# A planned attention and MLP block: LayerNorm in other VectorE forms, more time allowed for DMA transposes, score packs that may go out in halves

## The chip, the cores and the metric

One core of a Trainium2 chip. The metric is device time in microseconds (us). Most executions of one kernel agree within 0.3%. Engines: PE (TensorE), ACT (ScalarE), DVE (VectorE), POOL (GpSimd), SP (issues DMAs).

## The reference

```python
x = A_x                                             # 1 x 2048 x 640, bf16
h  = x + attention(layernorm(x), wq, wk, wv, wo)    # 32 heads of 20, one shared k and v
h2 = h + (gelu(ln(h) @ w_gate) * (ln(h) @ w_up)) @ w_down        # Df = 1536
```

Layernorm has no learned scale; eps is 1e-5. Attention is full: 32 heads x 2048 x 2048 scores.

## The kernel before

The program is written by a planner: it keeps an assumed clock for each engine, asks whichever engine is free first what to do next, and so fixes the order of every queue. What the chip runs is that order, with semaphores; the assumed times are gone. Two things follow. Every assumed duration changes the order, and a queue that was ordered for a too early arrival stands still behind it.

Scores are made in packs: four matmuls, one per 32-row group, each filling one PSUM bank (128 x 512). A tile of scores then goes one of two ways. ACT takes an exponential, one bank or two adjacent ones at a time. Or DVE writes a bit-pattern approximation ("DVE tile" below), which POOL completes with two shifted copies, so that it costs PE three value matmuls, not one.

```python
# a DVE instruction in a two-port mode and any POOL instruction exclude each other (the planner's view)
def commit(self, eng, fn, cost, lat, ..., lock=False):
    ...
    if lock:
        for o in self.ops["pool"][-2:]:
            if o.t0 <= t0 < o.end:
                t0 = o.end
        self.port = t0 + cost
    elif eng == "pool":
        t0 = max(t0, self.port)

# LayerNorm: after bn_stats/bn_aggr -> mv[..., 0] mean, mv[..., 1] variance
dve(lambda e: e.tensor_copy(ln_vb[:, ln, sl], mv[:, ln, sl, 1]), 80, ...)
dve(lambda e: e.tensor_scalar_add(ln_veb[:, ln, sl], ln_vb[:, ln, sl], EPS), 80, ...)
# ... POOL: pow 0.5; DVE: reciprocal ...
tk = _Task(("dve",), None, 320, L_DVE, keys + [("lr", kk)], [], prio, then, gate)
tk.lock = True
tk.fn = lambda e: e.tensor_scalar(xn_tmp[:, s, :], xh[:, t, :], mv[:, ln, t, 0:1],
                                  ln_r[:, ln, t:t + 1], ALU.subtract, ALU.mult)
sp_tasks.append(_Task(("sp",), lambda e: e.dma_start_transpose(o, xn_tmp[:, s, :]), 1330, 1700, ...))

# POOL stays idle up to YIELD ns for a locked DVE task that is about to be ready
if YIELD and state["kv_left"] == 0 and plan.free["dve"] < t + YIELD: ...   # for tk in tasks: if tk.lock ...

# a pack of scores needs four free banks; n of its four tiles go to DVE
if cand and len(ok) >= 4:
    issue_qk(t, cand[0], cand[1], ok)
# in issue_qk:
elif Dv > TH0: n = 0
elif Dv < SP2D[ph] and len(pend[1]) + len(pend[2]) < 2 * SP2P[ph] and (
        stall(t, 1, fb) + 1382.0 - stall(t, 2, fb) - 956.0 > SP2G[ph]): n = 2
else: n = 1
```

The softmax here doesn't subtract the row's maximum and nothing guards it: scores larger than these inputs give would overflow.

Of the kernel before, what the change touches and what calls it, by code (L numbers as in the profile page):

```python
# [9 lines left out]
P = 128  # L10
_DEBUG = {}
# [208 lines left out]
def bass_sequential_preLN__grouped_kv_mqa__glu_gated_geglu__prompt_kernel(  # L220
# [38 lines left out]
    EVF = 0  # L259
    EVW = 200.0  # L260
# [7 lines left out]
    NQ = 4  # L268
    NXT = 4
# [21 lines left out]
    qT = sb("qT", [P, NQ, 512], BF16)  # L291
    kT4 = sb("kT4", [P, S], BF16)
# [18 lines left out]
    ln_vb = sb("ln_vb", [P, 2, NT], BF16)  # L311
    ln_veb = sb("ln_veb", [P, 2, NT], BF16)
    ln_denb = sb("ln_denb", [P, 2, NT], BF16)
# [39 lines left out]
    SP2P = (3, 3, 3)  # L353
    SP2G = (300.0, 300.0, 300.0)
# [17 lines left out]
    YIELD = 500.0  # L372
    WQA = 1
    W_LAT = 3000.0
    ADDW = 100.0
# [7 lines left out]
    load("sp", xh[:, 0, :], x_view[:, 0, :], [("x", 0)], 2000)  # L383
# [19 lines left out]
    pool(lambda e: e.memset(halfc[:], 0.5), 40, writes=["halfc"])  # L403
    pool(lambda e: e.memset(wk4[:].bitcast(F32), 0.0), 300, writes=["wk4z"])
# [12 lines left out]
    state = {"mode": "m", "tab": "exp", "npack": 0, "exps_left": 2048, "misc_ready": False, "kv_left": NT, "qk_left": 512}  # L417
    bank_owner = {b: None for b in range(8)}
    slots = {"xt": list(range(NXT)), "q": list(range(NQ)), "onT": list(range(4)), "osb": [0, 1], "rcp": [0, 1], "onr": [0, 1]}
# [26 lines left out]
    def ln_group(ln, tiles, prio, done):  # L446
# [5 lines left out]
        def after_stats(op):  # L452
            cnt[0] += 1
            if cnt[0] == n:
                dve(lambda e: e.tensor_copy(ln_vb[:, ln, sl], mv[:, ln, sl, 1]), 80,
                    [("mv", ln, t) for t in tiles], [("vb", kk)], prio, c2)

        def c2(op):
            dve(lambda e: e.tensor_scalar_add(ln_veb[:, ln, sl], ln_vb[:, ln, sl], EPS), 80,
                [("vb", kk)], [("veb", kk)], prio, c3)  # L460

        def c3(op):
            task(("pool",), lambda e: e.tensor_tensor(ln_denb[:, ln, sl], ln_veb[:, ln, sl], halfc[:, 0:n], ALU.pow),
                 780, L_POOL, [("veb", kk), "halfc"], [("den", kk)], prio, c4)

        def c4(op):
            dve(lambda e: e.reciprocal(ln_r[:, ln, sl], ln_denb[:, ln, sl]), 90, [("den", kk)], [("lr", kk)],
                prio, c5)
# [5 lines left out]
        def norm(t):  # L474
# [9 lines left out]
            def then(op):  # L484
# [19 lines left out]
                sp_tasks.append(_Task(("sp",), lambda e: e.dma_start_transpose(o, xn_tmp[:, s, :]), 1330, 1700,  # L504
# [3 lines left out]
            tk = _Task(("dve",), None, 320, L_DVE, keys + [("lr", kk)], [], prio, then, gate)  # L508
            tk.lock = True

            def bind():
                s = start()
                tk.fn = lambda e: e.tensor_scalar(xn_tmp[:, s, :], xh[:, t, :], mv[:, ln, t, 0:1],  # L513
                                                  ln_r[:, ln, t:t + 1], ALU.subtract, ALU.mult)
                tk.writes = [("xt", s)]
# [73 lines left out]
    def kv_job(tiles):  # L589
# [24 lines left out]
        def vthen(b):  # L614
# [3 lines left out]
            def vfin(op):  # L618
                free_bank(b)
                for w in (1, 2):  # L620
                    task(("pool",), (lambda w: lambda e: e.tensor_scalar(
                        v_ext[:, t0:t0 + nt, w, 0:Dh], v_ext[:, t0:t0 + nt, 0, 0:Dh], CH_W[w], None, ALU.mult))(w),
# [25 lines left out]
    def q_job(u):  # L648
# [17 lines left out]

        def gate():
            if u["q"] is None:
# [9 lines left out]
        jb = _Job(("q", u["id"]), 1.0, pieces, then, gate)  # L678
        jobs.append(jb)
# [41 lines left out]
    def on_job(u, so):  # L721
# [13 lines left out]
        tk = _Task(("sp",), None, 1330, 1500, [("osb", so)], [], 0.5, None, lambda: bool(slots["onr"]))  # L735
# [26 lines left out]
    def on_transpose(t):  # L762
        sl = []
        tk = _Task(("sp",), None, 1330, 1500, [("onq", onslot[t], g) for g in range(NG)], [], 1.0, None,
# [327 lines left out]
    def stall(t, n, fb):  # L1092
# [21 lines left out]
        return max(0.0, free[3] + 460.0 - ta)  # L1114
# [5 lines left out]
    def issue_qk(t, u, kt, fb):  # L1120
# [21 lines left out]
        rr = [(k + i) % 4 for i in range(4)]  # L1142
        bk = {}
        tiles = {}
        want = (4 - n) // 2 if n != 2 or PAIR2 else 0
# [11 lines left out]
        ns = 4 - n - 2 * len(units_a)  # L1157
# [33 lines left out]
        u["npk"] += 1  # L1191
        u["left"].remove(kt)
        u["todo"] += 4 + 2 * n
        if not u["left"]:
            u["closed"] = True
            slots["q"].append(u["q"])
        state["npack"] += 1
        _DEBUG.setdefault("joblog", []).append((t, ("qk", u["id"])))
# [100 lines left out]
    def pe_decide(t):  # L1299
        cand = next_pack(t)  # L1300
# [3 lines left out]
        if cand and len(ok) >= 4:  # L1304
            issue_qk(t, cand[0], cand[1], ok)
            return True

        tq = 1e12
        if cand:
# [10 lines left out]
            tq = est[3] if len(est) > 3 else 1e12  # L1320
        lim = max(tq, act_end() - 570.0)
# [69 lines left out]
    def next_piece(t):  # L1391
# [26 lines left out]
        for jb in jobs:  # L1418
            pr = jb.prio
            if jb.name[0] == "q":  # L1420
                ahead = jb.name[1] - cur
                pr = 0.2 if ahead <= 0 else (0.9 if ahead <= 1 else 8.0 + 0.01 * ahead)
            if best is not None and pr >= best[0]:
                continue
# [19 lines left out]
    def issue_piece(t, jb, pc):  # L1444
        if isinstance(jb, _Start):
# [6 lines left out]
            if jb.name[0] == "q":  # L1452
                units[jb.name[1]]["q"] = slots["q"].pop(0)
        b = jb.bank
# [141 lines left out]
    def dve_decide(t):  # L1596
        imm = 1e12
        if dve_q:
# [7 lines left out]
            ev = None  # L1606
            if EVF and len(dve_q) <= EVF and x["vis"] > t - EVW:
                ev = next((tk for tk in tasks if tk.engs[0] == "dve" and any(k in (("b", 6), ("b", 7)) for k in tk.reads) and (
                    tk.gate is None or tk.gate()) and known(tk) and plan.ready("dve", tk.reads, tk.writes) <= t + 20), None)
            if ev is not None and x["vis"] <= t + 30:  # L1610
                tasks.remove(ev)
                run_task(t, ev, "dve")
                return True
# [225 lines left out]
```

## Time and profile before

| | before |
|---|---|
| median of runs, us | 789.38 (788.01 to 790.28); 788.69 with the run beside the changed kernel |
| profiled span, us | 785.8 |
| score tiles through ACT / through DVE | 1424 / 624 |
| filler matmuls (no useful result) | 428 |

The prediction below shows the page. The time from 13.5 us, about the first exponential, to the end of the last one is "attention", and the rest "tail", in which PE finishes the MLP.

### The profile page before, as it was taken

To read this page: it belongs to the slowest core of one execution; us is meant where nothing else is said; L and a number is where in the kernel's file an instruction comes from. 1 tells how busy PE (TensorE), PEld (TensorE's weight loads), DVE (VectorE), ACT (ScalarE), POOL (GpSimd) and SP (SyncE) were. 2 spreads that over 40 slices of the span, in tenths; PEclk is the share of its full clock that TensorE was granted. 3 is DMA by queue.
4 is the path that set the end of the run, shared out by engine and by line. 5 is a ranking of instruction groups with operands and counts; after the bars stand their busy time and mean duration, and the time that the engine had idled before them with its cause. 6 is when DMAs were issued, how large, how long until landed. Compare 5 with 4: busy or idle time off the path is not lost.

```text
span 785.8 us, 29885 instructions
## 1 busy us (share of the span) xinstructions
PE 703.4 (90%) x13140; PEld 333.0 (42%) x13140; DVE 610.9 (78%) x1096; ACT 730.3 (93%) x1058; POOL 660.8 (84%) x713
## 2 busy tenths in 40 slices
PE   5688888988889998999888899999998999989998
PEld 3332333432335453454234444445543444434467
DVE  7768878778888777877787777777788786878854
ACT  5799999999999998999999999999999999999981
POOL 5489998999999898888998989789898898889760
PEclk9999999999999999999999999999999999999999
DMA  6554401000110002100010002200021000110000
GB/s 196 86 127 148 109 8 25 19 10 8 25 26 9 3 26 27 26 26 8 9 26 19 9 10 43 26 26 3 10 43 25 9 3 18 35 25 18 11 20 18
DMA packets 56770, 25.90 MB, mean 33 GB/s; under 512 B 47809, under 2 KB 55361, under 8 KB 56641
## 3 DMA queue, kind: packets, MB, share of 16 engines
q1 hardware_dynamic: 55328, 23.55, 13.9%
q8 instruction: 105, 1.72, 0.9%
q10 hardware_dynamic: 1312, 0.44, 0.3%
q14 instruction: 25, 0.20, 0.1%
HBM read 10.21 MB, written 2.62 MB: 16 GB/s over the span
## 4 chain that ended last, share of the span: by engine, by line
PE 54%; ACT 23%; DVE 17%; DMA 4%; issue 2%; POOL 1%
PE ps L565 20%; ACT pa L1519 18%; PE ps L1256 15%; PE ps L1177 15%; DVE pd L1620 9%; PE ps L561 3%; ACT gbuf L905 3%; DVE xn_tmp L513 1%; DVE osb L1283 1%; PE ps L1382 1%; DVE stats L443 1%; DMA onr<-osb 1%; ACT L1519 1%; ACT L905 1%; DMA xh<-in_A_x_dram 1%
## 5 line engine op out<-in xcount | busy, mean ns | idle before, releaser
L1519 ACT ACTIVATE pa<-ps 128x512 bf16<-128x512 f32 (+1 forms) x1011 | 684.8, 814 | 27.0 <-PE ps L1177 21.8
L1586 POOL TENSOR_TENSOR pd<-pd,shifts 128x512 int32<-128x512 int32 x577 | 588.1, 1039 | 75.5 <-DVE pd L1620 70.4
L1620 DVE TENSOR_SCALAR pd<-ps 128x512 uint16<-128x512 f32 x624 | 417.7, 687 | 138.4 <-PE ps L1177 129.7
L1256 PE MATMUL ps<-pd,v_ext 128*32 128x512 bf16 x1872 | 286.4, 385 | 18.4 <-DVE osb L1283 11.9
L1256 PE MATMUL ps<-pa,v_ext 128*32 128x512 bf16 x1424 | 258.1, 386 | 4.4 <-ACT pa L1519 2.0
L1177 PE MATMUL ps<-qT,kT 32*128 32x512 bf16 x2048 | 203.3, 385 | 39.7 <-DVE pd L1620 22.9
L1177 PEld LDWEIGHTS ps<-qT,kT 32*128 32x128 bf16 x2048 | 56.1, 91 | 205.2 <-DVE pd L1620 126.6
L1256 PEld LDWEIGHTS ps<-pd,v_ext 128*32 128x32 bf16 x1872 | 78.3, 95 | 79.5 <-issue 33.4
L1256 PEld LDWEIGHTS ps<-pa,v_ext 128*32 128x32 bf16 x1424 | 70.2, 95 | 43.2 <-issue 22.1
L565 PE MATMUL ps<-xn2T,wg_sb 128*32 128x256 bf16 (+1 forms) x1736 | 68.3, 273 | 1.6 <-DMA xn2T<-xn_tmp 0.8
L565 PE MATMUL ps<-xn2T,wu_sb 128*32 128x256 bf16 x1680 | 67.2, 274 | 2.0 <-DVE gbuf L922 1.5
L565 PE MATMUL ps<-wd_sb,gbuf 128*32 128x320 bf16 x1344 | 66.3, 301 | 0.0
L565 PE MATMUL ps<-xn1T,wq_pad 128*32 128x256 bf16 (+1 forms) x1440 | 51.3, 266 | 0.8 <-POOL wq_pad L988 0.6
L565 PEld LDWEIGHTS ps<-xn2T,wg_sb 128*32 128x32 bf16 x1736 | 43.0, 96 | 20.6 <-issue 12.5
L565 PEld LDWEIGHTS ps<-xn2T,wu_sb 128*32 128x32 bf16 x1680 | 42.9, 96 | 20.9 <-issue 9.5
L565 PEld LDWEIGHTS ps<-wd_sb,gbuf 128*32 128x32 bf16 x1344 | 34.4, 96 | 23.9 <-issue 11.6
L922 DVE TENSOR_TENSOR gbuf<-ps,gbuf 128x512 bf16<-128x512 f32 x48 | 32.8, 682 | 9.7 <-PE ps L561 6.4
L565 PEld LDWEIGHTS ps<-xn1T,wq_pad 128*32 128x32 bf16 x1440 | 33.5, 98 | 15.4 <-issue 7.5
L1382 PE MATMUL ps<-kT,zz 128*32 128x512 bf16 x428 | 39.6, 396 | 0.0
L1568 POOL TENSOR_TENSOR pd<-pd,shifts 128x256 int32<-128x256 int32 x47 | 31.5, 687 | 0.0
L443 DVE BATCH_NORM_STATS2 stats<-xh 128x6 f32<-128x320 bf16 x64 | 29.8, 475 | 1.5 <-DMA xh<-in_A_x_dram 1.0
L565 PE MATMUL ps<-wo_sb,onT 128*32 128x320 bf16 x600 | 28.9, 301 | 1.4 <-DMA onT<-onq 1.1
(73 smaller groups left out, 348.0 us busy)
## 6 DMA issues: line engine op xcount, KB each, us to landing
out_dram<-xh SPq DMA_DIRECT2D x16, 160.0 KB, 1.8
xh<-in_A_x_dram SPq DMA_DIRECT2D x3, 640.0 KB, 6.3
wd_sb<-in_B_w_down_dram SPq DMA_DIRECT2D x4, 480.0 KB, 3.9
wg_sb<-in_B_w_gate_dram SPq DMA_DIRECT2D x3, 384.0 KB, 3.1
wu_sb<-in_B_w_up_dram SPq DMA_DIRECT2D x3, 384.0 KB, 3.0
wg_sb<-in_B_w_gate_dram SPq DMA_DIRECT2D x1, 768.0 KB, 4.3
wu_sb<-in_B_w_up_dram SPq DMA_DIRECT2D x1, 768.0 KB, 4.5
wo_sb<-in_A_wo_dram SPq DMA_DIRECT2D x1, 480.0 KB, 3.5
```

The costliest lines, as they stand in the source:

```text
L443: dve(lambda e: e.bn_stats(stats[:, ln, t, 6 * h:6 * h + 6], xh[:, t, h * HALF:(h + 1) * HALF]), 395, [key], [("st", ln, t, h)], prio, c)
L561: return e.matmul(o(b), l, r, start=st, stop=sp)
L565: ins = e.matmul(o(b)[a, :], l[:, a], r, start=st, stop=sp, tile_position=(0, 32 * j))
L905: task(("act",), (lambda v: lambda e: e.activation(v, v, ACT.Gelu_apprx_tanh))(v), ("gelu", c_act(n * (f1 - f0))), L_ACT, ks, ks, 1.0, (la ...
L922: dve(lambda e: e.tensor_tensor(o, i, o, ALU.mult), c_dve(n * k), [("b", bk)] + ks, ks, 1.0, fin)
L1177: ins = e.matmul(bank(b), kT4[32 * r:32 * r + 32, kt * P:(kt + 1) * P], qT[32 * r:32 * r + 32, s, :], start=True, stop=True, tile_position ...
L1256: ins = e.matmul(ps[32 * r:32 * r + 32, ab * 512:(ab + 1) * 512], v_ext[:, it["kt"], it["w"], :], it["ap"], start=st, stop=(j in ends), ti ...
L1382: ins = e.matmul(ps[32 * r:32 * r + 32, ab * 512:ab * 512 + n * P], zz[:], kT4[:, 0:n * P], start=False, stop=False, tile_position=(0, 32 ...
L1519: op = plan.commit("act", lambda e: e.activation(dst, src, ACT.Exp, scale=SM_SCALE), cost, L_ACT, [("b", b0 + i) for i in range(n)], [("pa ...
L1568: return e.tensor_tensor(pd32[:, w, h], pd32[:, 0, h], shifts[:, w - 1:w].to_broadcast([P, 256 * k]), ALU.add)
L1586: return e.tensor_tensor(pd32[:, 1:3, h], pd32[:, 0, h].unsqueeze(1).to_broadcast([P, 2, 256 * k]), shifts[:].unsqueeze(2).to_broadcast([P ...
L1620: op = plan.commit("dve", lambda e: e.tensor_scalar(pd[:, 0, s * 512:(s + 1) * 512], bank(b), CH_A, CH_B, ALU.mult, ALU.add), c_dve(512), ...
```

## The change

Its intent: keep LayerNorm's small DVE instructions out of the modes that exclude POOL, and drop the planner's care for that; allow for late transposes; and feed ACT when only two banks are free. The core of the diff (spilling queries to DRAM is added but switched off by `QD = 99` with 32 units; an early-eviction switch that was 0 is removed; the score routine is split into helpers; a few assumed costs change, as of the first load of x and of POOL's power; all that is cut). `stall`, the estimate behind the two-tile rule, asks when three banks are free instead of four while there is little other PE work (`SIX`).

```diff
+    HALF_ON = 1
+    HGAIN = 150.0
+    HBEG = 20
+    SIX = 2
+    LIGHT = 10
...
-    SP2P = (3, 3, 3)
-    SP2G = (300.0, 300.0, 300.0)
+    SP2P = (4, 4, 4)
+    SP2G = (200.0, 200.0, 200.0)
...
-    YIELD = 500.0
+    YIELD = 700.0
+    T_LAT = (1700.0, 2700.0, 2700.0)
-    ADDW = 100.0
+    ADDW = 60.0
...
-                dve(lambda e: e.tensor_copy(ln_vb[:, ln, sl], mv[:, ln, sl, 1]), 80,
+                narrow(ln_vb[:, ln, sl, 0], mv[:, ln, sl, 1:2], ...)
+        def narrow(o, i, reads, writes, then):
+                    return e.tensor_reduce(o, i, mybir.AxisListType.X, ALU.add)
-            dve(lambda e: e.tensor_scalar_add(ln_veb[:, ln, sl], ln_vb[:, ln, sl], EPS), 80,
+            narrow(ln_ve[:, ln, sl], ln_vb[:, ln, sl, :], ...)      # variance and eps, side by side
...
-                sp_tasks.append(_Task(("sp",), lambda e: e.dma_start_transpose(o, xn_tmp[:, s, :]), 1330, 1700,
+                sp_tasks.append(_Task(("sp",), lambda e: e.dma_start_transpose(o, xn_tmp[:, s, :]), 1330, T_LAT[ln],
...
-            tk = _Task(("dve",), None, 320, L_DVE, keys + [("lr", kk)], [], prio, then, gate)
-            tk.lock = True
+            tk = _Task(("dve",), None, 420, L_DVE, keys + [("lr", kk)], [], prio, then, gate)
-                tk.fn = lambda e: e.tensor_scalar(xn_tmp[:, s, :], xh[:, t, :], mv[:, ln, t, 0:1],
+                tk.fn = lambda e: e.tensor_scalar(xn_tmp[:, s, :].rearrange("p (a b) -> p a b", a=5), xh[:, t, :], mv[:, ln, t, 0:1],
...
-        return max(0.0, free[3] + 460.0 - ta)                                # in stall()
+        return max(0.0, free[SIX if light(t) else 3] + 460.0 - ta)
...
-        if cand and len(ok) >= 4:
+        if half is not None:
+            if len(ok) >= 2:
+                issue_half(t, half[0], half[1], half[2], ok, None)
+                return True
+        elif cand and len(ok) >= 4:
...
+            elif HALF_ON and len(ok) >= 2 and light(t) and tq + 445.0 - act_end() > HGAIN and state["npack"] > HBEG and state[
+                    "tab"] == "exp":
+                issue_half(t, cand[0], cand[1], [k % 4, (k + 1) % 4], ok, [(k + 2) % 4, (k + 3) % 4])
```

More of the change, by code (lines that the diff above doesn't have):

```diff
@@ L258, in bass_sequential_preLN__grouped_kv_mqa__glu_gated_geglu__prompt_kernel @@
     PH = (8, 99)
-    EVF = 0
-    EVW = 200.0
     PE_T1 = (0, 1)
@@ L268, in bass_sequential_preLN__grouped_kv_mqa__glu_gated_geglu__prompt_kernel @@
     NQ = 4
+    HALF_ON = 1
[3 more added lines that the diff above has]
+    LIGHT = 10
+    HD0 = 1300.0
+    HP0 = 3
+    QD = 99
+    QHOLD = 1
+    QAHEAD = 2
+    QPRI = 6.0
+    NQS = 2
     NXT = 4
@@ L291, in bass_sequential_preLN__grouped_kv_mqa__glu_gated_geglu__prompt_kernel @@
     qT = sb("qT", [P, NQ, 512], BF16)
+    qs = sb("qs", [P, NQS, 512], BF16)
+    qdr = nc.dram_tensor("q_scratch", [2 * NT, P, 512], BF16, kind="Internal").ap()
     kT4 = sb("kT4", [P, S], BF16)
@@ L310, in bass_sequential_preLN__grouped_kv_mqa__glu_gated_geglu__prompt_kernel @@
     mv = sb("mv", [P, 2, NT, 2], F32)
-    ln_vb = sb("ln_vb", [P, 2, NT], BF16)
-    ln_veb = sb("ln_veb", [P, 2, NT], BF16)
-    ln_denb = sb("ln_denb", [P, 2, NT], BF16)
+    ln_vb = sb("ln_vb", [P, 2, NT, 2], BF16)
+    ln_ve = sb("ln_ve", [P, 2, NT], BF16)
+    ln_den = sb("ln_den", [P, 2, NT], BF16)
     ln_r = sb("ln_r", [P, 2, NT], F32)
@@ L381, in load @@
         return plan.commit(eng, (lambda e: e.dma_start(o, i)), 480.0, lat, reads=after, writes=key, dma=True)
-    load("sp", xh[:, 0, :], x_view[:, 0, :], [("x", 0)], 2000)
+    load("sp", xh[:, 0, :], x_view[:, 0, :], [("x", 0)], 2750)
     load("act", wk_sb[:], cview(A_wk), ["wk"], 2500)
@@ L403, in bass_sequential_preLN__grouped_kv_mqa__glu_gated_geglu__prompt_kernel @@
     pool(lambda e: e.memset(halfc[:], 0.5), 40, writes=["halfc"])
+    pool(lambda e: e.memset(ln_vb[:, :, :, 1:2], EPS), 60, writes=["eps"])
     pool(lambda e: e.memset(wk4[:].bitcast(F32), 0.0), 300, writes=["wk4z"])
@@ L416, in bass_sequential_preLN__grouped_kv_mqa__glu_gated_geglu__prompt_kernel @@
     sp_tasks = []
-    state = {"mode": "m", "tab": "exp", "npack": 0, "exps_left": 2048, "misc_ready": False, "kv_left": NT, "qk_left": 512}
+    state = {"mode": "m", "tab": "exp", "npack": 0, "exps_left": 2048, "misc_ready": False, "kv_left": NT, "qk_left": 512, "half": None}
     bank_owner = {b: None for b in range(8)}
-    slots = {"xt": list(range(NXT)), "q": list(range(NQ)), "onT": list(range(4)), "osb": [0, 1], "rcp": [0, 1], "onr": [0, 1]}
+    slots = {"xt": list(range(NXT)), "q": list(range(NQ)), "onT": list(range(4)), "osb": [0, 1], "rcp": [0, 1], "onr": [0, 1], "qs": list(range(NQS))}
     pa_free = [True] * NA
@@ L454, in after_stats, with fn @@
             if cnt[0] == n:
-                dve(lambda e: e.tensor_copy(ln_vb[:, ln, sl], mv[:, ln, sl, 1]), 80,
-                    [("mv", ln, t) for t in tiles], [("vb", kk)], prio, c2)
+                narrow(ln_vb[:, ln, sl, 0], mv[:, ln, sl, 1:2], [("mv", ln, t) for t in tiles], [("vb", kk)], c2)
+        def narrow(o, i, reads, writes, then):
+            def fn(e):
+                with nc.allow_low_precision("one or two terms, rounded once"):
+                    return e.tensor_reduce(o, i, mybir.AxisListType.X, ALU.add)
+            dve(fn, 80, reads, writes, prio, then)
         def c2(op):
-            dve(lambda e: e.tensor_scalar_add(ln_veb[:, ln, sl], ln_vb[:, ln, sl], EPS), 80,
-                [("vb", kk)], [("veb", kk)], prio, c3)
+            narrow(ln_ve[:, ln, sl], ln_vb[:, ln, sl, :], [("vb", kk), "eps"], [("ve", kk)], c3)
         def c3(op):
-            task(("pool",), lambda e: e.tensor_tensor(ln_denb[:, ln, sl], ln_veb[:, ln, sl], halfc[:, 0:n], ALU.pow),
-                 780, L_POOL, [("veb", kk), "halfc"], [("den", kk)], prio, c4)
+            task(("pool",), lambda e: e.tensor_tensor(ln_den[:, ln, sl], ln_ve[:, ln, sl], halfc[:, 0:n], ALU.pow),
+                 690, L_POOL, [("ve", kk), "halfc"], [("den", kk)], prio, c4)
         def c4(op):
-            dve(lambda e: e.reciprocal(ln_r[:, ln, sl], ln_denb[:, ln, sl]), 90, [("den", kk)], [("lr", kk)],
+            dve(lambda e: e.reciprocal(ln_r[:, ln, sl], ln_den[:, ln, sl]), 90, [("den", kk)], [("lr", kk)],
                 prio, c5)
@@ L621, in vfin @@
                     task(("pool",), (lambda w: lambda e: e.tensor_scalar(
-                        v_ext[:, t0:t0 + nt, w, 0:Dh], v_ext[:, t0:t0 + nt, 0, 0:Dh], CH_W[w], None, ALU.mult))(w),
+                        v_ext[:, t0:t0 + nt, w, 0:Dh], v_ext[:, t0:t0 + nt, 0, 0:Dh], CH_W[w], 0.0, ALU.mult, ALU.add))(w),
                         180 + 75 * nt, L_POOL, [("v", t, 0) for t in tiles] + [("vone", w)],
@@ L665, in then, with then_far, fin @@
             flex_copy(qT[:, s, :], bank(b), 512, [("b", b)], [("q", s)], 0.6, fin)
+        def then_far(b):
+            s = u["qs"]
+            def fin(op):
+                free_bank(b)
+                sp_tasks.append(_Task(("sp",), lambda e: e.dma_start(qdr[u["id"]], qs[:, s, :]), 480, 2000,
+                                      [("qs", s)], [("qd", u["id"])], 0.4, lambda op2: slots["qs"].append(s)))
+                q_load(u)
+            flex_copy(qs[:, s, :], bank(b), 512, [("b", b)], [("qs", s)], 0.6, fin)
         def gate():
+            if u["id"] >= QD:
+                return bool(slots["qs"]) and (not QHOLD or state["kv_left"] == 0 or u["id"] - cur_unit() <= QAHEAD + 1)
             if u["q"] is None:
@@ L676, in gate, with q_load, bind, then @@
             return True
-        jb = _Job(("q", u["id"]), 1.0, pieces, then, gate)
-        jobs.append(jb)
+        if u["id"] >= QD:
+            jobs.append(_Job(("qd", u["id"]), QPRI, pieces, then_far, gate))
+        else:
+            jobs.append(_Job(("q", u["id"]), 1.0, pieces, then, gate))
+    def q_load(u):
+        tk = _Task(("sp",), None, 480, 2000, [("qd", u["id"])], [], 0.1, None)
+        def gate():
+            return bool(slots["q"]) and all(v["q"] is not None for v in units[:u["id"]]) and (
+                u["id"] - cur_unit() <= QAHEAD)
+        def bind():
+            s = slots["q"].pop(0)
+            u["q"] = s
+            tk.writes = [("q", s)]
+            tk.fn = lambda e: e.dma_start(qT[:, s, :], qdr[u["id"]])
+        def then(op):
+            u["qop"] = op
+        tk.gate = gate
+        tk.born = bind
+        tk.then = then
+        sp_tasks.append(tk)
+    def cur_unit():
+        return min([u["id"] for u in units if u["left"]] or [99])
     def normed(u, so, v, key, done):
@@ L734, in on_job @@
             return
-        tk = _Task(("sp",), None, 1330, 1500, [("osb", so)], [], 0.5, None, lambda: bool(slots["onr"]))
+        tk = _Task(("sp",), None, 1330, T_LAT[2], [("osb", so)], [], 0.5, None, lambda: bool(slots["onr"]))
         sl = []
@@ L763, in on_transpose @@
         sl = []
-        tk = _Task(("sp",), None, 1330, 1500, [("onq", onslot[t], g) for g in range(NG)], [], 1.0, None,
+        tk = _Task(("sp",), None, 1330, T_LAT[2], [("onq", onslot[t], g) for g in range(NG)], [], 1.0, None,
                    lambda: bool(slots["onT"]))
@@ L1141, in issue_qk, with issue_half, light, issue_rows @@
         k = state["npack"]
-        rr = [(k + i) % 4 for i in range(4)]
+        return issue_rows(t, u, kt, [(k + i) % 4 for i in range(4)], n, fb, False)
+    def issue_half(t, u, kt, rows, fb, more):
+        A = max(act_end() - t, 0.0)
+        Dv = dve_load(t)
+        nf = pd_free.count(True) - len(dve_q)
+        if A > 3000.0:
+            n = 2
+        elif Dv > TH0:
+            n = 0
+        elif Dv < HD0 and len(pend[1]) + len(pend[2]) < 2 * HP0:
+            n = 1
+        else:
+            n = 0
+        n = max(0, min(n, nf))
+        return issue_rows(t, u, kt, rows, n, fb, more)
+    def light(t):
+        n = sum(len(j.pieces) - j.pos for j in active)
+        for j in jobs:
+            if all(k in plan.w for k in j.pieces[0][2]) and (j.gate is None or j.gate()):
+                n += len(j.pieces)
+        return n <= LIGHT
+    def issue_rows(t, u, kt, rr, n, fb, more):
+        nr = len(rr)
         bk = {}
         tiles = {}
-        want = (4 - n) // 2 if n != 2 or PAIR2 else 0
+        want = (nr - n) // 2 if not (nr == 4 and n == 2) or PAIR2 else 0
         fb = list(fb)
@@ L1156, in issue_qk @@
         fb.sort(key=lambda b: ((b ^ 1) in fb, b))
-        ns = 4 - n - 2 * len(units_a)
+        ns = nr - n - 2 * len(units_a)
         dbanks = [fb.pop(0) for _ in range(n)]
@@ L1190, in issue_qk @@
             act_q.append(("S" if len(e) == 1 else "P", [tiles[r] for r, b in e]))
-        u["npk"] += 1
-        u["left"].remove(kt)
-        u["todo"] += 4 + 2 * n
+        u["todo"] += nr + 2 * n
+        _DEBUG.setdefault("joblog", []).append((t, ("qk", u["id"])))
+        if more or nr == 4:
+            u["npk"] += 1
+            u["left"].remove(kt)
+        if more:
+            state["half"] = (u, kt, more)
+            return op
         if not u["left"]:
@@ L1196, in issue_qk @@
             slots["q"].append(u["q"])
+        state["half"] = None
         state["npack"] += 1
-        _DEBUG.setdefault("joblog", []).append((t, ("qk", u["id"])))
         state["qk_left"] -= 1
@@ L1299, in pe_decide @@
     def pe_decide(t):
-        cand = next_pack(t)
+        half = state["half"]
+        cand = half or next_pack(t)
         piece = next_piece(t)
@@ L1320, in pe_decide @@
             tq = est[3] if len(est) > 3 else 1e12
+            if half is not None:
+                tq = est[1] if len(est) > 1 else 1e12
+            elif HALF_ON and len(ok) >= 2 and light(t) and tq + 445.0 - act_end() > HGAIN and state["npack"] > HBEG and state[
+                    "tab"] == "exp":
+                k = state["npack"]
+                state["nhalf"] = state.get("nhalf", 0) + 1
+                issue_half(t, cand[0], cand[1], [k % 4, (k + 1) % 4], ok, [(k + 2) % 4, (k + 3) % 4])
+                return True
         lim = max(tq, act_end() - 570.0)
@@ L1422, in next_piece @@
                 pr = 0.2 if ahead <= 0 else (0.9 if ahead <= 1 else 8.0 + 0.01 * ahead)
+            elif jb.name[0] == "qd":
+                pr = 0.5 if jb.name[1] - cur <= QAHEAD + 1 else QPRI + 0.01 * jb.name[1]
             if best is not None and pr >= best[0]:
@@ L1453, in issue_piece @@
                 units[jb.name[1]]["q"] = slots["q"].pop(0)
+            elif jb.name[0] == "qd":
+                units[jb.name[1]]["qs"] = slots["qs"].pop(0)
         b = jb.bank
@@ L1605, in dve_decide @@
                     break
-            ev = None
-            if EVF and len(dve_q) <= EVF and x["vis"] > t - EVW:
-                ev = next((tk for tk in tasks if tk.engs[0] == "dve" and any(k in (("b", 6), ("b", 7)) for k in tk.reads) and (
-                    tk.gate is None or tk.gate()) and known(tk) and plan.ready("dve", tk.reads, tk.writes) <= t + 20), None)
-            if ev is not None and x["vis"] <= t + 30:
-                tasks.remove(ev)
-                run_task(t, ev, "dve")
-                return True
             if x["vis"] <= t + 30 and s is not None:
```

## The prediction

> **What bounds the kernel now.** I read the busy shares first.
>
> ```profile
> PE 703.4 (90%) x13140; PEld 333.0 (42%) x13140; DVE 610.9 (78%) x1096; ACT 730.3 (93%) x1058; POOL 660.8 (84%) x713
> PE 54%; ACT 23%; DVE 17%; DMA 4%; issue 2%; POOL 1%
> ```
>
> The second line is the chain that ended last, by engine. PE leads it, but a share of the whole span mixes the head (LayerNorm, first keys), the long attention stretch and the MLP tail. The view by stretch separates them; its columns are PE, PEld, DVE, ACT and POOL busy, then clock and DMA.
>
> ```profile
> 40.00:760.00 720.00, 656.49 (x12307) 300.28 (x12304) 569.53 (x965) 697.67 (x1014) 638.64 (x662) 1.00 0.13 28
> ```
>
> In these 720 us ACT is busy 96.9%, PE 91%, POOL 89%, DVE 79%. ACT therefore sets the stretch; PE has 63 us without work, and 36 us of its busy time are filler matmuls (line 1382), which do no arithmetic for the result. ACT can only get shorter by waiting less, at most 22 us (720 - 697.7), or by doing less. The groups of instructions say what it does.
>
> ```profile
> L1519 ACT ACTIVATE pa<-ps 128x1024 bf16<-128x1024 f32 x413 | 437.9, 1065 | 1.8 <-PE ps L1177 1.4 <-PE ps L1256 0.3
> L1519 ACT ACTIVATE pa<-ps 128x512 bf16<-128x512 f32 x598 | 363.4, 640 | 25.2 <-PE ps L1177 20.4
> L1620 DVE TENSOR_SCALAR pd<-ps 128x512 uint16<-128x512 f32 x624 | 417.7, 687 | 138.4 <-PE ps L1177 129.7
> L1586 POOL TENSOR_TENSOR pd<-pd,shifts 128x512 int32<-128x512 int32 x577 | 588.1, 1039 | 75.5 <-DVE pd L1620 70.4
> ```
>
> Of 2048 score tiles, 2*413 + 598 = 1424 go through ACT's exponential and 624 (30.5%) through the DVE form, which POOL then completes with its adds. What stands between them is the split, chosen pack by pack when the program is generated. ACT's only big wait there is on the score matmuls:
>
> ```profile
> ACT pa L1519 <- PE ps L1177: 17.3, 46, 1.4
> PE ps L1177 <- DVE pd L1620: 22.9, 55, 1.0
> DVE rcp L696 <- DMA onr<-osb: 2.2, 4, 1.0
> ```
>
> (us in total, times, longest.) So 17.3 us of ACT's 22 are score matmuls that came late, and those in turn waited mostly for DVE to empty a bank.
>
> **What makes banks late.** LayerNorm's small DVE instructions show it, one- and two-tile groups of the same line:
>
> ```profile
> L513 DVE TENSOR_SCALAR xn_tmp<-xh,mv,ln_r 128x640 bf16<-128x640 bf16 x32 | 17.7, 572 | 0.1
> L455 DVE CAST ln_vb<-mv 128x2 bf16<-128x2 f32 x14 | 5.5, 391 | 0.1
> L459 DVE TENSOR_SCALAR ln_veb<-ln_vb 128x2 bf16<-128x2 bf16 x14 | 3.9, 280 | 0.1
> L455 DVE CAST ln_vb<-mv 128x1 bf16<-128x1 f32 x4 | 0.6, 150 | 0.1
> ```
>
> A cast of two elements takes 391 ns on average where one element takes 150. In order of time one of them reads so, DVE and then the POOL run beside it:
>
> ```profile
> 598.97 1.00 DVE L455 CAST ln_vb<-mv 128x2 bf16<-128x2 f32 x1
> 596.80 3.13 POOL L1586 TENSOR_TENSOR pd<-pd,shifts 128x512 int32<-128x512 int32 x3
> ```
>
> The cast ends at 599.97, when the third POOL add ends (599.93): it was held. ACT stands idle soon after, 0.75, 0.32 and 0.61 us before 605.08, 607.89 and 610.07.
>
> The second cause is transposes by DMA. The chain in order of time has four late ones in the attention stretch; the last two lines are ACT afterwards.
>
> ```profile
> 138.14 4.29 DMA xn2T<-xn_tmp
> 303.09 4.36 DMA onT<-onq
> 344.68 3.94 DMA onr<-osb
> 504.21 4.47 DMA onr<-osb
> 144.29 65.32 ACT L1519 ACTIVATE pa<-ps 128x512 bf16<-128x512 f32 x98 [1.25 <-PE ps L1177]
> 308.74 19.81 ACT L1519 ACTIVATE pa<-ps 128x512 bf16<-128x512 f32 x28 [1.36 <-PE ps L1177]
> ```
>
> The generator orders each engine's queue with an assumed 1330 + 1500 or 1700 ns per transpose, so 2.8 to 3.0 us; these took 3.9 to 4.5. PE's queue is in order, so a matmul placed for the assumed time blocks the scores behind it.
>
> **What the Trainium skill says.** "SBUF — State Buffer", in its section on the engine and DMA sides: the port pair shared by DVE and GpSimd is an exclusive lock for a whole instruction, and the loser blocks. The trace agrees (1.00 us against 0.15). "VectorE: DVE Perf Modes", "What auto-detection actually checks": the two-port mode needs source and destination in SBUF with outermost dims both even or equal; 16-bit step-1 data still gets the packed one-port mode. The one-tile cast, outer dim 1, fits: 150 ns. "The perf-mode tier table" of that page has tensor_reduce at 1x only, so never two-port; with two elements that costs nothing, and no trace here shows it yet. "TensorEngine Tiling (Array Packing)", "Key Properties": different tiles run in parallel. The trace agrees: a pack of four score matmuls starts and ends together (385 ns each), so two of them should hold PE about as long as four.
>
> **The change part by part.**
>
> *LayerNorm forms.* The cast and the add of epsilon become reductions over one and two elements, the normalisation writes through a view of five blocks of 128 against a flat 640, so 5 against an even dim: no two-port mode, but packed. Fourteen casts by (391 - 150) ns is 3.4 us; fourteen adds by (280 - 150) is 1.8; the 16 norms in the stretch average 9.96/16 = 623 ns against 458 in the head (7.33/16), where some are alone at 430: 16 * 0.19 = 3.1. About 8 us leave DVE, which is not the bound. On the end counts only what ACT lost: the idle gaps of ACT just after such held instructions (around 222, 411, 602 and 688 us) add up to 4.2 us. The lock bookkeeping for norms goes too, so the rule that held POOL back for a norm no longer fires. I book -4 us.
>
> *Slack for transposes.* 2700 ns instead of 1500 or 1700 makes 4.03 us, above most transposes and just below the four late ones. ACT's gaps after these are 1.25, 1.36, 0.27 and 0.46 us: -3 us. The last transposes of the kernel go by PE, so the tail barely pays for the slack.
>
> *Half packs.* With two free banks, little other PE work and ACT otherwise dry, two of four score rows go out. Of the 17.3 us, 17.3 - 4.2 - 3.3 = 9.8 remain; gaps are 0.2 to 0.6 us each, and the rule wants light work. I take half: -4.5 us. Cost: a second pass of about 0.2 us on PE (a quarter pack's four tiles hide together) for perhaps 40 to 60 halves, 8 to 12 us out of PE's 63 idle and 36 filler.
>
> *Split.* Two DVE tiles in a pack are allowed with one more add waiting (4, not 3), a gain of 200 instead of 300 ns, and pending adds weigh 60, not 100. Halves may take one DVE tile in two. All push tiles from ACT to DVE. ACT's rate: 1424/1011 = 1.41 tiles per activation and 12 activations in an unbroken 8.12 us, so 0.677/1.41 = 0.48 us per tile. I estimate 16 more DVE tiles: -7.7 us on ACT; +10 us on DVE (0.65 each in a run), about what LayerNorm gave back; +17 us on POOL, to 656 of about 706 us, 93%; a few us on PE. POOL's share is why I don't book more.
>
> *Dead parts.* The early-eviction switch was 0; the spill of queries to DRAM starts at unit 99 of 32. They cost nothing.
>
> Sum: 4 + 3 + 4.5 + 7.7 = 19.2 us. The gains overlap (a half pack fills the gap that a held cast would have left) and a reordered plan gets new gaps, so I book about three quarters: -14 us, 775.5 us, 1.8%.
>
> **The rivals.** (a) POOL becomes the bound: it already runs 89%. If the split moves 40 tiles, POOL needs 42 us more and would be full; its adds come late, PE waits for pd, the gain shrinks to 6-8 us: 782. Against it: POOL still idles 70 us behind DVE evictions. (b) PE becomes the bound: halves double the score pass, and PE is the largest share of the chain. With 150 halves, 30 us of PE go; result 783 to 790. Against it: the rule for light work, and fillers that give way. (c) Everything converts: 20 us or more, about 768, if the tuned split moves more than 16 tiles and gaps close.
>
> **Range and chances.** 765 to 786: below lies (c) with a larger split, above (a) or (b). The 2% line is at 773.6, close to my figure: 0.41 faster, 0.57 within, 0.02 slower; every part is aimed at a wait that the trace has.
>
> **What would show it.** Casts near 150 ns and norms at 430 to 460 ns with none over 0.6; no transpose with more than 0.5 us of PE behind it; ACT's wait on scores in the stretch from 17 to under 10 us; 635 to 655 DVE evictions; POOL above 91% there. Wrong would be: the DVE tiles unchanged (then no gain beyond waits, 780), the count of filler matmuls unchanged with PE's own waits grown (rival b), or ACT below 95% busy there (rival a).

## More of the kernel before

View by stretch of the kernel before; columns: length, then busy us of PE, PEld, DVE, ACT, POOL, then clock, DMA share, GB/s.

```profile
13.50:759.45 745.95, 673.71 (x12658) 308.37 (x12654) 590.81 (x1039) 718.72 (x1039) 652.26 (x687) 0.99 0.14 29
759.45:785.80 26.35, 23.56 (x363) 20.31 (x360) 10.36 (x22) 6.28 (x10) 2.06 (x3) 1.00 0.05 15
```

ACT is idle 745.95 - 718.72 = 27.2 us of attention. In the tail no PE group shows idle time before it until the last matmul; PE is working off what attention left over.

## The result, and the profile after

Median 776.19 us (775.46 to 776.84, 4 runs) beside 788.69 for the kernel before; ratio 0.9846, 95% interval 0.9814 to 0.9877. The prediction said 775.5.

The page of the changed kernel, busy shares and chain by engine:

```profile
PE 709.2 (92%) x12913; PEld 336.3 (43%) x12913; DVE 614.9 (79%) x1112; ACT 723.7 (93%) x1079; POOL 667.1 (86%) x723
PE 56%; ACT 29%; DVE 12%; DMA 2%; issue 1%; DVEq 0%
```

DVE went from 17% to 12% of the chain and DMA from 4% to 2%. Attention and tail, columns as before:

```profile
13.50:745.78 732.28, 677.49 (x12447) 310.04 (x12447) 593.94 (x1054) 711.28 (x1058) 660.07 (x698) 0.99 0.14 30
745.78:775.00 29.22, 26.44 (x347) 22.45 (x344) 11.07 (x24) 6.88 (x11) 1.05 (x2) 1.00 0.07 24
```

Attention is 13.7 us shorter: ACT is busy 7.4 us less (718.7 to 711.3) and idle 6.2 us less (27.2 to 21.0). The tail is 2.9 us **longer**. So the span of the two profiled runs gained 10.8 (the medians differ by 12.5). The groups that answer to those shown before, shapes kept apart (the exponential is line 1625 now, the DVE form 1718, the POOL adds 1692):

```profile
L1625 ACT ACTIVATE pa<-ps 128x1024 bf16<-128x1024 f32 x380 | 405.1, 1070 | 4.8 <-PE ps L1261 2.4 <-PE ps L1345 2.3
L1625 ACT ACTIVATE pa<-ps 128x512 bf16<-128x512 f32 x652 | 384.7, 653 | 15.5 <-PE ps L1261 10.6 <-PE ps L1345 0.4
L1718 DVE TENSOR_SCALAR pd<-ps 128x512 uint16<-128x512 f32 x636 | 422.1, 687 | 121.7 <-PE ps L1261 113.7
L1692 POOL TENSOR_TENSOR pd<-pd,shifts 128x512 int32<-128x512 int32 x586 | 595.7, 1040 | 60.9 <-DVE pd L1718 57.2 <-DVE ln_vb L475 0.9
L475 DVE TENSOR_REDUCE ln_ve<-ln_vb 128x2 bf16<-128x4 bf16 x14 | 2.0, 145 | 0.1
L475 DVE TENSOR_REDUCE ln_vb<-mv 128x2 bf16<-128x2 f32 x14 | 2.0, 143 | 0.0
L532 DVE TENSOR_SCALAR xn_tmp<-xh,mv,ln_r 128x640 bf16<-128x640 bf16 x32 | 20.1, 651 | 0.2
```

Twelve tiles moved to DVE (624 to 636). The cast and the add fell from 391 and 280 ns to 143 and 145. The normalisation did **not** get shorter: 572 ns before, 651 now. In order of time, DVE and then POOL:

```profile
591.48 2.11 DVE L532 TENSOR_SCALAR xn_tmp<-xh,mv,ln_r 128x640 bf16<-128x640 bf16 x2
590.29 3.11 POOL L1692 TENSOR_TENSOR pd<-pd,shifts 128x512 int32<-128x512 int32 x3
```

Two normalisations take 2.11 us and end just after the third POOL add (593.40), which is the held cast of the kernel before over again. ACT's wait for scores in the stretch from 40 to 750 us (us, times, longest):

```profile
ACT pa L1625 <- PE ps L1261: 8.9, 28, 1.4
```

It was 17.3 us in 46 waits. The four late transposes are gone from the chain; of that length only one of the first LayerNorm is left (4.24 us at 19.26), whose assumed landing the change leaves at 1700 ns. Counted at the planner's own calls while the program is built, 54 of 512 packs went out in halves; filler matmuls fell from 428 to 288.

### The profile page after: what moved, and what is told of

It reads as the page before. It is cut to its first block, busy times and chain, and to the rows that moved or that the text cites. A ratio compares the mean times of both kernels' runs of the same rounds, so it can differ in the third digit from the quotient of the medians.

```text
span 775.0 us, 29498 instructions
## 1 busy us (share of the span) xinstructions
PE 709.2 (92%) x12913; PEld 336.3 (43%) x12913; DVE 614.9 (79%) x1112; ACT 723.7 (93%) x1079; POOL 667.1 (86%) x723
## 4 chain that ended last, share of the span: by engine, by line
PE 56%; ACT 29%; DVE 12%; DMA 2%; issue 1%; DVEq 0%
ACT pa L1625 25%; PE ps L584 21%; PE ps L1345 16%; PE ps L1261 15%; DVE pd L1718 6%; PE ps L580 3%; ACT gbuf L962 2%; DVE xn_tmp L532 2%; DVE osb L1372 1%; DMA xn1T<-xn_tmp 1%; DVE stats L457 1%; DMA xh<-in_A_x_dram 1%; PE ps L1484 1%; ACT L1625 1%; ACT L962 1%
## 5 line engine op out<-in xcount | busy, mean ns | idle before, releaser
L1692 POOL TENSOR_TENSOR pd<-pd,shifts 128x512 int32<-128x512 int32 x586 | 595.7, 1040 | 60.9 <-DVE pd L1718 57.2
L1718 DVE TENSOR_SCALAR pd<-ps 128x512 uint16<-128x512 f32 x636 | 422.1, 687 | 121.7 <-PE ps L1261 113.7
L1345 PE MATMUL ps<-pd,v_ext 128*32 128x512 bf16 x1908 | 294.6, 384 | 15.4 <-DVE osb L1372 11.6
L1261 PE MATMUL ps<-qT,kT 32*128 32x512 bf16 x2048 | 221.1, 386 | 32.2 <-DVE pd L1718 15.2
L1261 PEld LDWEIGHTS ps<-qT,kT 32*128 32x128 bf16 x2048 | 61.2, 91 | 203.5 <-DVE pd L1718 108.4
L1345 PEld LDWEIGHTS ps<-pd,v_ext 128*32 128x32 bf16 x1908 | 81.1, 95 | 77.2 <-issue 33.0
L584 PE MATMUL ps<-xn2T,wg_sb 128*32 128x256 bf16 x1680 | 65.6, 274 | 0.6 <-DVE gbuf L935 0.5
L584 PE MATMUL ps<-wd_sb,gbuf 128*32 128x320 bf16 x1252 | 61.8, 301 | 0.1
L935 DVE CAST gbuf<-ps 128x512 bf16<-128x512 f32 x42 | 28.8, 687 | 1.3 <-PE ps L584 0.9
```

The costliest lines, as they stand in the source:

```text
L584: ins = e.matmul(o(b)[a, :], l[:, a], r, start=st, stop=sp, tile_position=(0, 32 * j))
L935: dve(lambda e: e.tensor_copy(o, i), c_dve(n * k), [("b", bk)], ks, 1.0, fin)
L1261: ins = e.matmul(bank(b), kT4[32 * r:32 * r + 32, kt * P:(kt + 1) * P], qT[32 * r:32 * r + 32, s, :], start=True, stop=True, tile_position ...
L1345: ins = e.matmul(ps[32 * r:32 * r + 32, ab * 512:(ab + 1) * 512], v_ext[:, it["kt"], it["w"], :], it["ap"], start=st, stop=(j in ends), ti ...
L1692: return e.tensor_tensor(pd32[:, 1:3, h], pd32[:, 0, h].unsqueeze(1).to_broadcast([P, 2, 256 * k]), shifts[:].unsqueeze(2).to_broadcast([P ...
L1718: op = plan.commit("dve", lambda e: e.tensor_scalar(pd[:, 0, s * 512:(s + 1) * 512], bank(b), CH_A, CH_B, ALU.mult, ALU.add), c_dve(512), ...
```

## The experiments

Each but r7 was timed in five rounds beside the kernel before, four to a call. "Split" is the two-tile rule and its weight (`SP2P`, `SP2G`, `ADDW`). The calls ran on three chips (r1 to r4, r5 to r8, r9 to r12), so across calls the ratios compare better than the medians. Attention and tail are read from one profile each, as above; r10's profile is its fastest run, 2.3 us below its median. DVE tiles are counts in the built programs, split packs the planner's calls while building. The expectations give smaller numbers of split packs (32, 36, 65): they were counted from a listing in which two halves that follow each other at once look like one whole pack. The table's numbers fit the traces: per split pack the score matmuls' busy time is 0.30 to 0.35 us above the kernel before in every run with halves. Every run keeps the fifth part of the change (`SIX`) and the small assumed costs, so "old" below does not mean the kernel before in every line.

| run | LayerNorm | slack | split | halves | median us | ratio, 95% interval | attention | tail | DVE tiles | split packs |
|---|---|---|---|---|---|---|---|---|---|---|
| before | old | old | old | off | 787 to 788 | 1 | 745.95 | 26.35 | 624 | 0 |
| r1 (the change) | new | new | new | on | 776.89 | 0.986 (0.9842-0.9878) | 732.20 | 29.20 | 636 | 54 |
| r2 | new | new | new | **off** | 786.94 | 0.9987 (0.9969-1.0005) | 741.90 | 30.10 | 640 | 0 |
| r3 | new | new | **old** | on | 775.54 | 0.9846 (0.983-0.9863) | 729.55 | 30.45 | 633 | 44 |
| r4 | new | **old** | new | on | 780.7 | 0.9926 (0.9904-0.9948) | 732.24 | 32.36 | 637 | 53 |
| r5 | **old** | new | new | on | 783.86 | 0.9959 (0.9937-0.998) | 738.40 | 31.40 | 640 | 50 |
| r6 | order of new, **old casts** | new | new | on | 778.62 | 0.9887 (0.9868-0.9906) | 733.35 | 29.25 | 636 | 54 |
| r8 | new | 2800 | new | on | 774.96 | 0.9842 (0.9821-0.9863) | 727.85 | 30.05 | 638 | 52 |
| r9 | old | old | old | on | 789.33 | 1.0028 (1.0009-1.0047) | 740.63 | 34.17 | 633 | 57 |
| r10 | new | old | old | off | 780.85 | 0.9912 (0.9895-0.993) | 734.64 | 28.56 | 637 | 0 |
| r11 (wrong result) | norm truly one-port | new | new | on | 772.75 | 0.9818 (0.98-0.9837) | 728.17 | 29.23 | 636 | 54 |
| r12 | new | new | new | **more** | 781.96 | 0.9936 (0.9917-0.9955) | 726.32 | 41.88 | 638 | 117 |

The theory at the start was the prediction's sum: the parts act separately, each by the ACT gaps it closes. The rivals: one part carries everything, or the parts are redundant.

**r1**, the changed kernel again.

> The changed kernel again, as the mark for the three others of this call. Both theories: 776 us, ratio to the kernel before 0.984 plus or minus 0.003.

As expected.

**r2**, half packs off.

```diff
-    HALF_ON = 1
+    HALF_ON = 0
```

> Half packs off, all else as changed; the plan then has no split pack (32 packs were split), 640 DVE tiles instead of 636, 388 filler matmuls instead of 288. Theory of parts (the prediction's sum): the half packs carry 3 to 5 us, so 779 to 781 us, and ACT's wait on scores in the stretch grows from 9 to about 13 us. Rival, half packs carry the whole gain: 786 or more. Rival, redundant (another rule fills the same gaps): within 1.5 us of the changed kernel.

The rival's number: 10 us lost, nearly the whole gain, although this plan has four more DVE tiles than the change. Attention in r2, columns as before, and PE's wait for DVE to empty a bank from 40 to 745 us:

```profile
13.50:755.40 741.90, 673.22 (x12565) 309.02 (x12556) 600.43 (x1062) 712.76 (x1040) 663.79 (x699) 1.00 0.14 29
PE ps L1261 <- DVE pd L1718: 26.4, 69, 0.9
```

ACT's idle time is 741.90 - 712.76 = 29.1 us, against 21 with halves; its busy time is within 1.5 us of the change's. So in this company half packs act on waits, as meant: scores wait 26.4 us for DVE's banks without them and 15.2 with them, and ACT's wait on scores is 12.8 us without them, as the theory of parts said, against 8.9. But r10, also without half packs, has a wait of 9.4, so that sign alone does not speak for them.

**r3**, the split parameters back.

```diff
-    SP2P = (4, 4, 4)
-    SP2G = (200.0, 200.0, 200.0)
-    ADDW = 60.0
+    SP2P = (3, 3, 3)
+    SP2G = (300.0, 300.0, 300.0)
+    ADDW = 100.0
```

> The three split parameters back (3, 300 ns, weight 100), all else as changed; the plan has 633 DVE tiles instead of 636. Theory of parts: the prediction gave the split 7.7 us for 16 tiles; with only 3 tiles between these two plans that allows 1.5 us (3 times 0.48), so 777 to 779 us. Rival: the split parameters act through the order rather than the count and 5 us or more go (781 or above).

Below either expectation: not slower at all. The new split parameters bring nothing here. Yet 633 of the 636 DVE tiles are still there, so they do not hang on these parameters (more under r10).

**r4**, the transposes' assumed landing back.

```diff
-    T_LAT = (1700.0, 2700.0, 2700.0)
+    T_LAT = (1700.0, 1500.0, 1500.0)
```

> The assumed landing of the LayerNorm-2 and attention transposes back to 1500 ns (LayerNorm 2 had 1700), all else as changed. Theory of parts: 3 us go, 778 to 780 us, and the chain of waits shows late transposes (3.9 to 4.5 us) in the attention stretch again, with ACT idle about 1.3 us after each that PE waits for. Rival, the waits were hidden by other work: within 1.5 us of the changed kernel and no late transpose in the chain.

Four us slower, and the late transposes are in the chain again; six of them, of 3.2 to 4.4 us, three shown:

```profile
268.27 4.41 DMA onr<-osb
314.22 4.38 DMA onr<-osb
...
706.03 4.05 DMA onT<-onq
```

The second half of the expectation failed as a rule: ACT stands idle 1.14 us after the first of these (before 274.89), but around 314 us it works without a gap, and attention is as long as in r1 (732.24 and 732.20). The loss is in the tail, 3.2 us longer, with 96 full-width down-projection matmuls in it instead of 71. That fits PE having done less MLP work during attention, but one plan cannot show that the late transposes alone did it.

**r5**, LayerNorm wholly as before, planner's bookkeeping included.

```diff
+            tk.lock = True                    # and cost 320, YIELD 500
-                narrow(...) twice, five-block view
+                tensor_copy, tensor_scalar_add, flat view
```

> LayerNorm wholly as before (cast, add of epsilon and flat normalisation, the lock bookkeeping, the 320 ns estimate, the 500 ns yield), all else as changed; its plan has 640 DVE tiles. Theory of parts: 4 us go, so about 780 us. Theory after the first four runs (half packs carry the gain, the other parts only fill the same gaps or the tail): 776 to 779 us.

783.86, worse than both expectations. LayerNorm is worth about 7 us here, not 4 and not nothing.

**r6**, only the instructions' form, every queue in the order of the changed kernel.

```diff
-                narrow(ln_vb[:, ln, sl, 0], mv[:, ln, sl, 1:2], ...)
+                dve(lambda e: e.tensor_copy(ln_vb[:, ln, sl, 0], mv[:, ln, sl, 1]), 80, ...)
-            narrow(ln_ve[:, ln, sl], ln_vb[:, ln, sl, :], ...)
+            dve(lambda e: e.tensor_scalar_add(ln_ve[:, ln, sl], ln_vb[:, ln, sl, 0], EPS), 80, ...)
```

> The very same order of every queue as the changed kernel, only the cast and the add of epsilon issued in their old forms. Casts and adds of two elements should again average 300 to 400 ns with single ones of 1 us, beside the POOL adds. Prediction's step (held casts cost ACT time): 2 to 3 us longer, 778 to 779. Rival, DVE has room for them: within 1 us of the changed kernel.

```profile
L469 DVE CAST ln_vb<-mv 128x2 bf16<-128x2 f32 x14 | 5.0, 356 | 0.0
L479 DVE TENSOR_SCALAR ln_ve<-ln_vb 128x2 bf16<-128x2 bf16 x14 | 4.8, 341 | 0.1
```

Held again, and about 2 us slower than r1 by the medians (1.2 us by the two profiled spans; the two intervals overlap), as the prediction's step said. The order is the same, so what there is of it is the form alone. The remaining 5 us between r5 and r6 go with the order that the lock bookkeeping and its assumed costs make; each is one plan.

**r7**, why the normalisation is still held (wrong result).

```diff
-                ... xh[:, t, :], mv[:, ln, t, 0:1], ln_r[:, ln, t:t + 1], ALU.subtract, ALU.mult)
+                ... xh[:, t, :], 0.0, 20.0, ALU.subtract, ALU.mult)
```

> Wrong result on purpose: the normalisation keeps its five-block output view and its place in the order, but takes two constants instead of the two per-partition scalars from SBUF. In the changed kernel it is still held beside POOL adds (up to 1245 ns, 440 when alone). If the scalars from SBUF are what takes the shared port: no instance above 0.5 us. If the view does not keep it off the two-port mode: instances of 0.9 to 1.2 us remain in the attention stretch.

Instances in the stretch from 40 us on, ns at least/median/most:

```profile
L532 DVE TENSOR_SCALAR xn_tmp<-xh x16: 261/700/1162, 145.6 to 755.2; 128x640 bf16<-128x640 bf16 x16
```

Still held, up to 1162 ns, so the scalars are not the reason. And 261 ns for 640 elements is too short for two elements a cycle (640/1.92 = 333 ns at the 0.96 GHz of the Trainium skill's "VectorE: DVE Perf Modes", Specifications; an estimate): it ran four at a time, the two-port mode. The built program says why. The five-block view of a contiguous row is merged into one run of 640 before it reaches the chip; writing the same kernel with the flat view gives the identical instruction. This part of the change changes nothing.

**r8**, a change without intent.

```diff
-    T_LAT = (1700.0, 2700.0, 2700.0)
+    T_LAT = (1700.0, 2800.0, 2800.0)
```

> Assumed landing of transposes 2800 instead of 2700 ns: a change with no intent, to see how far the time moves when the plan is merely another one. 638 DVE tiles, the same 32 split packs. If plans are interchangeable: within 1 us of the changed kernel. If the plan is chaotic: 2 to 4 us either way, most of it in the tail, as matmuls of the down projection left after the last exponential.

About 2 us below r1 by the medians, with overlapping intervals: the first expectation's size or a little more. A difference of 2 us between two plans is not yet a cause.

**r9**, half packs alone, the three other named parts as before (r5's edit with r3's and r4's).

> Half packs alone: LayerNorm and its lock bookkeeping, the transposes' assumed landing and the three split parameters as before; 36 split packs, 633 DVE tiles. If half packs carry their 10 us by themselves: 776 to 779 us, ratio 0.987. If they need the other parts (a plan that knows when banks come free): 782 to 787, ratio 0.993 or above.

No gain at all: attention is 5.3 us shorter, the tail 7.8 us longer.

**r10**, LayerNorm alone of the four named parts (r2's, r3's and r4's edits together).

> LayerNorm alone (new forms, no lock bookkeeping), the other three parts as before; no split pack, 637 DVE tiles. The prediction booked 4 us (784 to 785). After the run without half packs, which had LayerNorm, slack and split and was at 0.9987: within 2 us of the kernel before, with any shorter attention given back in the tail.

7 us faster, more than the prediction's 4 and against the expectation taken from r2. ACT's wait on scores from 40 to 745 us and attention, columns as before:

```profile
ACT pa L1625 <- PE ps L1261: 9.4, 35, 0.8
13.50:748.14 734.64, 669.95 (x12657) 309.03 (x12650) 595.48 (x1053) 713.43 (x1041) 661.00 (x697) 1.00 0.14 30
```

It has 637 DVE tiles with the old split parameters. What brings the tiles is not shown. It is not LayerNorm alone: r9 has the old LayerNorm and the old split parameters, and 633. Programs that were built to count tiles, but not run, show how fickle the count is. The fifth part moves it by 4 to 8: with `SIX = 3`, which is the old rule, r10 would have 629 and the changed kernel 632, and with all four named parts as before it is 633 with the fifth part and 625 without. The kernel before would have 631 with only the new split parameters, and also 631 with only another assumed time for the first load of x. What the fifth part is worth in time, no run tells; r10 has it, and so does r9, which gains nothing.

r4 has LayerNorm, half packs and split, and is no faster than r10 (780.7 and 780.85 us; ratios 0.9926 and 0.9912). r3, which has LayerNorm, half packs and slack, is 5 us faster (775.54). So in these plans half packs beside LayerNorm pay only with the slack; LayerNorm with slack alone was not run.

**r11**, a normalisation that cannot be merged (wrong result; same order of all queues).

```diff
-  e.tensor_scalar(xn_tmp[:, s, :].rearrange("p (a b) -> p a b", a=5), xh[:, t, :], ...)
+  e.tensor_scalar(xn_tmp[:, s, :].rearrange("p (a b) -> p a b", a=5)[:, :, 0:126], xh[:, t, 0:630], ...)
+  # and one memset of xn_tmp at the start
```

> Wrong result on purpose: same order of all queues, but the normalisation reads a run of 630 and writes five rows of 126 with gaps, which cannot be merged into one run as the view of five blocks of 128 was. If an odd outer count against an even one keeps an instruction off the shared port: all 32 at 430 to 480 ns, none held. Then DVE has 5 to 6 us less in the attention stretch, and the time tells what the normalisation step was worth: 1 to 3 us below the changed kernel if held instructions cost ACT time as the held casts did (about 2 us).

Instances from 40 us on, first of the changed kernel, then of r11:

```profile
L532 DVE TENSOR_SCALAR xn_tmp<-xh,mv,ln_r x16: 429/841/1245, 145.0 to 756.4; 128x640 bf16<-128x640 bf16 x16
```
```profile
L532 DVE TENSOR_SCALAR xn_tmp<-xh,mv,ln_r x16: 521/592/600, 145.3 to 752.3; 128x630 bf16<-128x630 bf16 x16
```

None is held any more. An undisturbed one costs more than expected (592, not 430 to 480), but the longest falls from 1245 to 600, and attention is 4.0 us shorter in the same order of work; the time is about 3 us below r1 (ratio 0.9818 against 0.986). What the change meant to do with the norm is worth that much; as written it does not do it. A correct version was not run.

**r12**, half packs under far looser conditions, 117 instead of 54.

```diff
-    LIGHT = 10
+    LIGHT = 40
```

> Half packs allowed with up to 40 pieces of other PE work waiting instead of 10: 65 split packs instead of 32, 224 to 220 filler matmuls instead of 288. If ACT's gaps are what they fill and gaps remain (about 10 us of waits on scores): 1 to 3 us faster, 773 to 775. If PE is the second bound: ACT's waits shrink but the second pass (33 more, 0.2 us each, 7 us) leaves more down-projection work for the tail, so the same or up to 4 us slower with a tail above 31 us.

The second expectation, more strongly: 5 us slower than r1 by the medians.

```profile
13.50:739.82 726.32, 679.71 (x12010) 300.99 (x12002) 592.97 (x1060) 706.41 (x1082) 651.43 (x699) 0.99 0.14 30
739.82:781.70 41.88, 38.52 (x475) 32.83 (x475) 16.37 (x34) 9.93 (x15) 0.66 (x2) 1.00 0.09 21
```

Attention is shorter again (726.3), ACT's idle time there is 19.9 us, and the tail is 12.7 us longer than in r1: PE is busy 38.5 us in it. The score matmuls hold PE 240.4 us, against 220.6 in r1. Whatever PE does not get done beside attention it does afterwards, alone.

## Why the prediction was right

The total and its main reading hold: attention ACT-bound, scores that wait for banks, a shift of tiles, -12.5 us measured and -14 predicted. Its list of signs: casts near 150 ns (143 and 145), ACT's wait below 10 us (8.9), 635 to 655 DVE tiles (636), POOL above 91% (647.16 us of the 710 from 40 to 750, 91.2%), none of the late transposes for which it allows more time: all as said, though r10, without half packs, slack or split, already has a wait of 9.4. The norms near 430 to 460 ns: not.

Term by term the sum did less well, and the errors cancelled, which is luck.

- **LayerNorm, booked 4 us.** It measured 7 us alone (r10, with the fifth part) and about 7 when undone (r5), so it was under-booked. The form of the casts is about 2 us (r6); the step "norms leave the shared port" failed, since the view never reached the chip, and would have been about 3 us more (r11); about 5 us go with the order that the planner's lock and its assumed costs make, which the prediction named and did not size.
- **Split, booked 7.7 us for 16 tiles.** Twelve tiles moved, and ACT's work on the exponential's line fell by 6.6 us in attention (691.2 to 684.6): the 0.48 us per tile was nearly right (12 x 0.48 = 5.8). But the cause was wrong: the parameters bring nothing (r3) and no tiles to speak of (633 without them); by the counts under r10, each of several changes moves a plan by 4 to 8 tiles, one without intent included, so what brought the twelve stays open.
- **Slack, booked 3 us.** Undoing it costs about 4 (r4), but in the tail, not as the ACT gaps that the prediction added up.
- **Half packs, booked 4.5 us.** In company they are worth 10 (r2), alone nothing (r9), and nothing, with the split, beside LayerNorm without the slack (r4 against r10). They are the least additive part. Their cost was under-booked: 54 lie in the expected 40 to 60, but the score matmuls' busy time rose from 203.3 to 221.1 us, 0.33 us each and not 0.2 (ends of matmuls are modelled in the profile). The prediction's own reading, that two matmuls hold PE about as long as four, says about 0.385.
- **Not booked: the tail.** The prediction treated PE's spare time in attention as free. It is the time in which the MLP is done; the tail took back 2.9 us of the 13.7. Rival (b) of the prediction, PE as the bound, is not what happened here, but it is real one step further (r12).

Two readings were wrong without harm. The casts of one element, set beside those of two as if the form were the difference, all began while POOL stood idle (one ends at 734.57, POOL's next add starts at 734.59), and in the first 40 us those of two elements take 0.15 to 0.18 us as well. So they are no evidence for "outer dim 1", all the less as 1 and 1 are equal. The add of epsilon is: with one element it takes 0.15 us at 735.08, within POOL's add of 734.59 to 735.63. And 4.03 us is not below all four late transposes, since one took 3.94.

The losses from undoing halves, LayerNorm and slack one at a time, about 10, 7 and 4 us, add up to more than the whole gain of 12, so the parts are not redundant but depend on each other. Why is only partly settled. A shorter attention stretch that PE did not use for the MLP shows in r9: half packs with the old bookkeeping gain 5.3 us and lose 7.8 in the tail. What stays open is why r2, which is r10 with slack and the new split added, is 6 us slower than r10. In the profiles its attention is 7.3 us longer (part of it because r10's profile is its fastest run), and ACT idles 29.1 us there, against 21.2 (734.64 - 713.43). So the 10 us of the half packs are measured against a plan that is itself poor; the three other parts together add 4 us to r10. Each cell of the table is a single plan, and r8 shows that a change without intent can move about 2 us, so part of these differences may be the luck of a plan. No run here separates that.

## What to carry to other kernels

When a generator orders the queues, its assumed durations and locks are part of the kernel: the order that came with dropping a lock went with more time here (5 us, one plan each) than the instruction forms that justified it (about 2 us). When parts are switched off one by one, look for a part of the diff that no switch turns off; here such a part (`SIX`) moves the count of DVE tiles, with which the split was credited. Before crediting a rewritten access pattern, look at the pattern in the built program and at the longest instance, not the mean. And in a stretch where one engine is the bound and another does later work in its gaps, count the tail: gains taken from those gaps come back there.

## What the Trainium skill lacked or had wrong

- "VectorE: DVE Perf Modes", What auto-detection actually checks: its rule agrees with r11 (five rows against an even run: 521 to 603 ns over all 32, never held). It lacks the warning that a view of contiguous data is merged before the chip sees it: the five-block view of 640 stayed in the two-port mode, 395 ns at the least and 1245 when held.
- The same page, The perf-mode tier table, gives no cost for scalars read from SBUF. With two constants a normalisation in the first 40 us took 320 ns in the median, with two per-partition scalars 440.
- "SBUF — State Buffer", on the shared port pair: that the loser waits for the whole instruction agrees (a two-element cast of 1.00 us beside a POOL add of 1.04, 0.14 us as a reduction). No page says what such waits cost the rest of a program: r11 saves 2 us of DVE busy time (20.1 to 18.1 on its line), 2 us of POOL's on its adds (596.3 in r1 to 594.2) and about 4 us of attention.
- No page gives the spread of DMA transposes that sit beside each other: the medians here were 2.5 to 2.9 us to landing, the late ones 3.9 to 4.5.
